# Backward of an adaLN block with a sliding-window decode attention and a gated feed-forward: part of the feed-forward's row sums moved from VectorE to TensorE

## The chip, the cores and the metric

The kernel runs on one core of one Trainium2 chip. The metric is the device time of one execution in microseconds; three executions of the kernel before took 605.77, 607.19 and 608.46 us, so its median is 607.19 us. The engines are named as the profile names them: PE is TensorE (PEld its weight loads), DVE is VectorE, ACT is ScalarE, POOL is GpSimd, SP is SyncE. POOL and SP here mainly issue DMAs.

## The reference, cut to what matters

The forward pass of one token (all tensors bf16, D = 1024, F = 3584, 32 query heads over 4 key/value heads of 128, a cache of 65,536 rows of which only the last W = 4096 are attended to):

```
mod = silu(c) @ w_mod                       -> sa, ca, ga, sb, cb, gb   (1024 each)
h   = layernorm(x) * (1 + ca) + sa
x   = x + ga * (attention(h, last 4096 rows of k, v) @ wo)
h   = layernorm(x) * (1 + cb) + sb
x   = x + gb * ((sigmoid(h @ w_gate) * (h @ w_up)) @ w_down)
```

The kernel must return x and the gradients, for a given grad_out, with respect to x, both caches, wq, wo, w_gate, w_up, w_down, c and w_mod. The gradients of the caches are as large as the caches, 61,440 of 65,536 rows of each head being zero: 120 pieces of about 1 MB of zeros are written, and these are called fills below. The gradients of the weight matrices are outer products of a column and a row, so most of the rest of the output is also plain writing.

In the feed-forward's backward pass the gradient of the hidden input is needed: dh2[j] = sum over f of (w_up[j, f] du[f] + w_gate[j, f] dg[f]), where du and dg are called the dug row. This is the row sum that the change deals with.

## The kernel before, in words

All of the work is written out by hand in one function, in the order in which each engine is to run it; each engine runs its own instructions strictly in that order and waits on semaphores of the others. Nearly all of SBUF is one tile, `arena`, cut by hand with `ar(off, size)`; a piece is used again as soon as its last reader is done, and for a stored piece that is when its DMA has landed.

DMAs leave by two queues: POOL issues most of them (fills, weights, gradients; the queue q0 of the profile), SP a few loads and stores (q1). Both queues run on the same 16 DMA engines. A fill is issued by `zero(n)` at the place where it is called; how many are issued at which place is set by the constants `Z_...` at the head of the file. There are 120 in all, so a fill that one place does not issue is issued at a later one.

The stages in order: modulation and query; scores; sums over the attended rows; the products called b_ps (a stage of 512 large matmuls); the feed-forward; a stage of outer products (`dw_rows`, `dwd`, `dwo`); and the gradients of keys, values, wq and w_mod.

The feed-forward (lines 1009 to 1152) goes over F in NB = 7 blocks q of 512. For each block, w_up and w_gate (2 MB, `load_ug`, two buffers, POOL queue) and w_down (1 MB, `load_wd`, one buffer, SP queue) are loaded. The work of a block is:

- `front(q)`, PE: 32 matmuls multiply the block's weights with the column h2_bf; the sums lie in a PSUM bank `fg` (`gu_ps` in its first half, the feed-forward's output `ffn_ps` in its second).
- `turn(q)`: `gates` (DVE masks and sums the PSUM rows into a column, clears `gu_ps` by a memset, ACT computes two sigmoids); `wd_ttr`: four DVE multiply-and-sum instructions over w_down (line 251); `hh_ops`: three small DVE products; `ffn_mm`, PE: 16 matmuls of w_down; then `load_wd(q + 1)`. `dug_part` ends it: two small DVE products make the dug column, PE spreads it into a row in PSUM (8 transposes, line 1059), and ACT copies that row to SBUF (`dug_b`, line 1060). DVE cannot go on before that copy has ended.
- the loop over j, DVE: eight multiply-and-sum instructions `ttr` of 128x1024 (line 251, out arena), one for each of the eight weight tiles of the block, each multiplied in place with `dug_b`. After the fourth, the first half of block q + 2 is loaded over the tiles that are done; after the eighth, the second half. Fills are issued beside both.

Beside this run 46 side jobs (`tr_unit`, line 910 and 911): eight PE transposes into a PSUM tile and an ACT copy back, for later stages. They are taken from a list by `side()`, one for each j. PE's PSUM tiles for the jobs and for the dug row are two, in turn.

In the last two blocks the gradient of w_down of earlier blocks is made too: `dwd(q, off, outer)` multiplies four rows of 128x1024 with columns, on ACT (`outer_act`) or on DVE (`outer_dve`), and stores 1 MB.

After the last block, in the order of the lines 1146 to 1170: `dwd(4)`, `dw_rows(0, 0)` (a 128x3584 product, stored as 0.9 MB), the column of the feed-forward's output from `ffn_ps`, dh2, `op_ps` (32 small matmuls in the same PSUM bank as `fg`), `dwd(5)`, the layer norm's backward (`layernorm_bwd_col`, with a PE sum over partitions between two DVE steps), `dattn_bf`, its broadcast (`bcast`), and then 64 matmuls with wo (line 1263) that give do. Only when do_bf is there do the eight `dwo` follow, each of which stores 1 MB; the `dw_rows` stand between them.

Of the kernel before, what the change touches and what calls it, by code (L numbers as in the profile page):

```python
# [10 lines left out]
P = 128  # L11
# [45 lines left out]
Z_FFN = [(1, 3), (1, 3), (2, 3), (1, 3), (1, 3), (2, 2), (0, 0)]  # L57
Z_HAND = (1, 1, 1, 0)
Z_ROWS = (1, 1)
@with_exitstack  # L60
def kernel(
# [44 lines left out]
    def vt(shape, name, dt=FP32):  # L106
        return pool.tile(shape, dt, name=name)
# [118 lines left out]
    def new_acc(name="acc"):  # L226
        return new_bank(name)[:, 0:64]
# [95 lines left out]
    def layernorm_bwd_col(dln, ln, rstd, name):  # L323
# [4 lines left out]
        means = total_bcast(part, 2, name + "_means", -1.0 / D)  # L328
# [119 lines left out]
    def heads(w):  # L448
        return w.rearrange("p (n d) -> p n d", d=P)
# [561 lines left out]
    dh2acc = vt([P, NB * KD], "dh2acc")  # L1011
# [6 lines left out]
    gu_ps, ffn_ps = fg[:, 0:256], fg[:, 256:512]  # L1018
# [13 lines left out]
    def gates():  # L1032
        rows_to_cols(gu_t, gu_ps, 8, gu_ps)
        nc.vector.memset(gu_ps, 0.0)
        nc.scalar.activation(out=small["sg"], in_=gu_t[:, 4:8], func=ACT.Sigmoid)
        nc.scalar.activation(out=small["om"], in_=gu_t[:, 4:8], func=ACT.Sigmoid, scale=-1.0)

# [15 lines left out]
    def dug_part(q):  # L1053
        dug = dug_all[:, 8 * q:8 * q + 8]
        mulv(dug[:, 0:4], small["dhh"], small["sg"])
        mulv(dug[:, 4:8], small["dhh"], small["hom"])
        tp = new_tp("tp_dug")
        for i in range(8):
            nc.tensor.transpose(tp[:, i * P:(i + 1) * P], dug[:, i:i + 1].broadcast_to([P, P]), ident_bf[:, :])  # L1059
        return nc.scalar.copy(out=dug_b.rearrange("p (k f i) -> p k f i", k=2, i=4),  # L1060
                              in_=tp.rearrange("p (k i f) -> p k f i", k=2, i=4))
# [44 lines left out]
    rot[:] = [(psum, "mm"), (prq, "rq")]  # L1106
    side(1)
    front(0)
    for n, ins in zip(Z_FOLD[2:], turn(0)):
        zero(n, ins)  # L1110
    side(2)
    for q in range(NB):
        z = Z_FFN[q]
        for j in range(KD):
            w = ug_v[:, q % 2, j // 4, j % 4, :, :].rearrange("p k f -> p (k f)")
            ttr(w, w, dug_b, dh2acc[:, q * KD + j:q * KD + j + 1])
            if j == 2 and q + 1 < NB:
                front(q + 1)
            if len(jobs) > 0:
                side()  # L1120
# [11 lines left out]
        if q == NB - 2:  # L1132
            store()
        zero(z[1])
        if q + 2 < NB:
            turn(q + 1)
        elif q + 1 < NB:
            stores = []
            turn(q + 1, lambda: stores.append(dwd(1, 40, outer_act)))
            stores[0]()  # L1140
            zero(Z_HAND[0])
            dwd(2, 152, outer_dve)()
            zero(Z_HAND[1])
            dug_rows(0)
    dwd(4, 32, outer_dve)()
    zero(Z_HAND[3])
# [3 lines left out]
    rows_to_cols(ffn, ffn_ps, KD, ffn_ps)  # L1150
    dh2 = vt([P, KD], "dh2")
    nc.vector.reduce_sum(out=dh2, in_=dh2acc.rearrange("p (b j) -> p j b", j=KD), axis=AX.X)
# [9 lines left out]
    dwd(5, 152, outer_dve)()  # L1162
    dx1b, m2 = layernorm_bwd_col(dln2, ln2, rstd2, "ln2b")
# [4 lines left out]
    dattn_b = scr  # L1168
    bcast(dattn_bf, KD, dattn_b, "V")
# [99 lines left out]
    dw_rows(0, 1, 16, outer_dve)  # L1269
# [11 lines left out]
    dw_rows(0, 2, 40, outer_dve)  # L1281
    dq_bf = vt([P, HQ], "dq_bf", BF16)
# [6 lines left out]
    zero(Z_ROWS[0])  # L1289
    dwo(3)  # L1290
    dw_rows(0, 5, 40, outer_dve)
    dw_rows(0, 6, 16, outer_dve)
    dwo(0)
# [12 lines left out]
    zero(Z_ROWS[1])  # L1306
# [10 lines left out]
    dw_rows(1, 2, 32, outer_dve)  # L1317
    dw_rows(1, 3, 40, outer_dve)
# [11 lines left out]
    dw_rows(1, 4, 16, outer_dve)  # L1330
    sec(1)
# [5 lines left out]
    dw_rows(1, 6, 40, outer_dve)  # L1337
    dw_rows(1, 7, 16, outer_dve)
# [114 lines left out]
```

## Time and profile before

| what | value |
|---|---|
| median of three executions | 607.19 us (605.77 to 608.46) |
| the profiled execution, device time | 604.81 us |
| its span, first to last instruction | 603.0 us |
| bytes moved by DMA | 246.49 MB, 409 GB/s over the span |
| busy share of the span, PE / DVE / ACT / POOL | 66% / 62% / 40% / 25% |
| feed-forward, from the first `gates` to the last row sum | 313.50 to 446.03 us |

The span lies inside the device time; 1.81 us of it lie around the span. In the views below, a line of the timeline gives start and length in us, engine, line of the kernel, operation, what it writes and reads, the count, and in brackets how long the engine had been idle before it and what ended that. Lines of line groups give the count, then busy time and mean length, then idle time before them. Lines by windows give the window, its length, and for each engine its busy time with the number of instructions, then TensorE's granted clock, the DMA engines' busy share (it can be above 1, as packets overlap) and the rate in GB/s.

### The profile page before, as it was taken

How to read it: one execution, taken by the hardware profiler on the slowest of the kernel's cores; microseconds unless marked ns; L12 is line 12 of the kernel's file. 1: busy time of each engine (PE TensorE's matmuls, PEld its weight loads, DVE VectorE, ACT ScalarE, POOL GpSimd, SP SyncE). 2: the span in 40 equal slices, each digit the busy share in tenths (PEclk: the TensorE clock that was granted, in tenths of full speed). 3: DMA queues.
4: the chain of work that ended last, by engine and by line, in shares of the span. 5: the costliest groups of instructions: out<-in, count | busy, mean ns of one | idle time of the engine just before them, and what ended most of it. 6: DMA issues, size and time to landing. Idle time of an engine off the chain costs nothing.

```text
span 603.0 us, 8913 instructions
## 1 busy us (share of the span) xinstructions
PE 396.1 (66%) x3556; PEld 224.4 (37%) x3556; DVE 371.4 (62%) x677; ACT 240.2 (40%) x382; POOL 151.6 (25%) x253
## 2 busy tenths in 40 slices
PE   3997789999999999979766544554226104665510
PEld 2784434334345456435434333343114104413100
DVE  3756499999411030293738888988696735696750
ACT  3489515557211034112235444554443223754410
POOL 3113113212222122222212323321211615233100
PEclk9997699999999999989987777786567656755555
DMA  8999999999999999999999999999996899999998
GB/s 349 421 418 422 414 453 413 433 431 431 409 427 403 456 435 393 447 430 421 388 414 390 408 411 414 418 414 417 425 408 258 336 417 410 424 416 417 413 414 334
DMA packets 33881, 246.49 MB, mean 409 GB/s; under 512 B 5697, under 2 KB 5697, under 8 KB 18448
## 3 DMA queue, kind: packets, MB, share of 16 engines
q0 software_dynamic: 29424, 225.99, 93.7%
q1 hardware_dynamic: 4368, 19.93, 9.2%
q8 instruction: 28, 0.46, 0.3%
q14 instruction: 13, 0.11, 0.0%
q10 hardware_dynamic: 48, 0.01, 0.0%
HBM read 78.28 MB, written 185.60 MB: 438 GB/s over the span
## 4 chain that ended last, share of the span: by engine, by line
PE 37%; DVE 25%; DMA 17%; issue 9%; ACT 7%; POOL 2%; ACTq 0%; POOLq 0%; DVEq 0%; SPq 0%
PE b_ps L767 16%; DMA arena<-in_B_w_down_dram 9%; DVE arena L234 6%; PE n_ps L710 6%; DMA out_dram<-arena 5%; DVE scr L251 5%; DVE arena L251 4%; DVE arena L247 4%; ACT arena L521 2%; ACT arena L1241 2%; PE t_ps L668 2%; DMA out_dram<-zeros 1%; PE tp_k L500 1%; PE w_ps L463 1%; PE ok L630 1%
## 5 line engine op out<-in xcount | busy, mean ns | idle before, releaser
L767 PE MATMUL b_ps<-arena 128*128 128x512 bf16 x512 | 118.6, 385 | 1.1 <-ACT arena L911 1.1
L911 ACT COPY arena<-tp_side 128x1024 bf16<-128x1024 bf16 x62 | 59.8, 1028 | 55.0 <-PE tp_side L910 55.0
L234 DVE TENSOR_TENSOR arena<-arena 128x2048 bf16<-128x2048 bf16 x64 | 76.5, 1223 | 2.3 <-PE n_ps L710 0.3
L251 DVE CUSTOM_DVE_ANT_0 arena<-arena,scr 128x1024 bf16<-128x1024 bf16 x56 | 64.7, 1222 | 13.4 <-ACT scr L1060 13.4
L767 PEld LDWEIGHTS <-arena 128*128 128x128 bf16 x512 | 49.3, 99 | 59.0 <-issue 5.9
L710 PE MATMUL n_ps<-arena 128*128 128x512 bf16 x256 | 65.6, 378 | 5.8 <-DVE arena L234 4.2
L201 POOL DMA_DIRECT2D out_dram<-out_dram x68 | 33.6, 495 | 116.5 <-PE n_ps L710 38.4
L910 PE MATMUL tp_side<-ident_bf,arena 128*128 128x128 bf16 x496 | 46.7, 253 | 16.0 <-ACT arena L911 7.9
L910 PEld LDWEIGHTS <-arena 128*128 128x128 bf16 x496 | 38.8, 116 | 25.7 <-issue 17.5
L247 DVE TENSOR_SCALAR arena<-arena,h 128x3584 bf16<-128x3584 bf16 (+1 forms) x24 | 28.8, 1201 | 25.8 <-DMA out_dram<-arena 25.7
L710 PEld LDWEIGHTS <-arena 128*128 128x128 bf16 x256 | 24.6, 97 | 41.2 <-issue 15.8
L1237 PE MATMUL ps_kv<-arena 32*128 32x512 bf16 x64 | 24.4, 588 | 20.5 <-DVE arena L255 11.1
L207 POOL DMA_DIRECT2D out_dram<-zeros x45 | 24.9, 559 | 50.4 <-PE q_ps L437 13.7
L251 DVE CUSTOM_DVE_ANT_0 scr<-arena,b1k 128x1024 bf16<-128x1024 bf16 x28 | 34.2, 1223 | 5.4 <-DMA arena<-in_B_w_down_dram 4.9
L1241 ACT ACTIVATE arena<-ps_kv 128x512 bf16<-128x512 f32 x48 | 25.4, 697 | 29.0 <-PE ps_kv L1237 28.8
L243 DVE CAST arena<-b_ps 128x512 bf16<-128x512 f32 x6 | 4.2, 692 | 50.8 <-PE b_ps L767 50.8
L670 ACT CAST arena<-t_ps 128x512 bf16<-128x512 f32 x56 | 30.1, 589 | 12.1 <-PE t_ps L668 12.1
L936 POOL DMA_DIRECT2D arena<-in_B_w_up_dram x14 | 10.8, 774 | 65.7 <-DVE dh2acc L251 38.3
L1060 ACT COPY scr<-tp_dug 128x1024 bf16<-128x1024 bf16 x7 | 7.1, 1012 | 46.0 <-PE tp_dug L1059 46.0
L1024 PE MATMUL fg<-arena,hh_bf 128*32 128x256 bf16 x112 | 5.9, 347 | 29.3 <-DVE hh_bf L234 29.3
L521 ACT COPY arena<-tp_wq 128x1024 bf16<-128x1024 bf16 x23 | 21.4, 1071 | 7.3 <-PE tp_wq L519 7.3
L1059 PE MATMUL tp_dug<-ident_bf,rows_all 128*128 128x128 bf16 x56 | 7.2, 311 | 24.0 <-DVE rows_all L234 24.0
(321 smaller groups left out, 639.5 us busy)
## 6 DMA issues: line engine op xcount, KB each, us to landing
out_dram<-zeros POOLq DMA_DIRECT2D x45, 1024.0 KB, 13.1
out_dram<-arena POOLq DMA_DIRECT2D x35, 1024.0 KB, 10.1
out_dram<-arena POOLq DMA_DIRECT2D x16, 896.0 KB, 9.8
arena<-in_A_wq_dram POOLq DMA_DIRECT2D x8, 1024.0 KB, 21.1
arena<-in_A_wo_dram POOLq DMA_DIRECT2D x8, 1024.0 KB, 12.3
arena<-in_w_mod_dram POOLq DMA_DIRECT2D x7, 1024.0 KB, 18.6
arena<-in_B_w_up_dram POOLq DMA_DIRECT2D x14, 512.0 KB, 9.1
arena<-in_B_w_gate_dram POOLq DMA_DIRECT2D x14, 512.0 KB, 9.6
```

What stands on the lines that cost most here:

```text
L201: ins = nc.gpsimd.dma_start(out=as_rows(region, BIGP).bitcast(FP32), in_=zero_src[:, 0:P * ZW // 4].rearrange("i (p x) -> (i p) x", p=BIGP ...
L207: ins = nc.gpsimd.dma_start(out=region.bitcast(FP32), in_=zeros[:, :])
L234: return nc.vector.tensor_tensor(out=out, in0=a, in1=b, op=op)
L247: return nc.vector.tensor_scalar(out=out, in0=a, scalar1=s1, scalar2=None, op0=op0)
L251: return nc.vector.tensor_tensor_reduce(out=out, in0=w, in1=b, scale=1.0, scalar=0.0, op0=ALU.mult, op1=ALU.add, accum_out=acc)
L521: nc.scalar.copy(out=blk, in_=tp[:, :])
L670: nc.scalar.copy(out=o, in_=ps)
L710: mm = nc.tensor.matmul(nbank[k][:, :], lhsT=k_nat[:, g, t_ * DH:(t_ + 1) * DH], rhs=vp[:, t_ % 2, 4 * k:4 * k + 4, :].rearrange("p h d -> ...
L767: mm = nc.tensor.matmul(bbank[p][k][:, :], lhsT=a4[:, p, h, :], rhs=wo_t[u][:, a, k * 512:(k + 1) * 512], start=(i == 0 and a == 0), stop= ...
L910: nc.tensor.transpose(tp[:, i * P:(i + 1) * P], blk[:, i * P:(i + 1) * P], ident_bf[:, :])
L911: nc.scalar.copy(out=blk if dst is None else dst, in_=tp[:, :])
L1241: nc.scalar.activation(out=o, in_=v, func=ACT.Copy, scale=float(scale))
```

## The change

Of each block's eight row sums, five (`JV = 5`) stay on DVE. For the other three, `turned(q)` transposes each weight tile on PE (24 transposes of 128x128), and ACT copies the result back over the tile in place; `turned_mm(q)` then multiplies the turned tiles with the dug column in 24 matmuls with one output column, which add up in a third part of the bank `fg`. The feed-forward's output is also taken with one-column matmuls (32 for each block in place of 16 of 256 columns), so that it needs no masking at the end. The dug row's copy is shared by ACT and DVE. ACT clears `gu_ps` in place of a DVE memset. `load_wd` goes in two halves of 512 KB, each issued when the half's rows have been used. The side jobs are taken two before `front`, three after it and one in `turn`. The three `dwd` that ACT computed go to DVE. In the part after the loop, `dwd(5)` moves into the layer norm's PE sum, and `dw_rows(0, 1)` ahead of the broadcast. Of the fills, the loop issues 17 and no longer 25, the `dwd` stores have one each (5 in place of 3), and the `dw_rows` eight in place of two.

```diff
-Z_FFN = [(1, 3), (1, 3), (2, 3), (1, 3), (1, 3), (2, 2), (0, 0)]
-Z_HAND = (1, 1, 1, 0)
-Z_ROWS = (1, 1)
+Z_FFN = [(0, 3)] * 5 + [(0, 2)]
+Z_HAND = (1, 1, 1, 1, 1)
+Z_ROWS = (1, 1, 1, 1, 1, 1, 1, 1)
+JV = 5
...
     def gates():
         rows_to_cols(gu_t, gu_ps, 8, gu_ps)
-        nc.vector.memset(gu_ps, 0.0)
         nc.scalar.activation(out=small["sg"], in_=gu_t[:, 4:8], func=ACT.Sigmoid)
         nc.scalar.activation(out=small["om"], in_=gu_t[:, 4:8], func=ACT.Sigmoid, scale=-1.0)
+        nc.scalar.activation(out=gu_ps.rearrange("p (n d) -> p n d", n=2), func=ACT.Copy, scale=0.0,
+                             in_=ident_f.rearrange("p (n d) -> p n d", n=1).broadcast_to([P, 2, P]))
+
+    def turned(q):
+        for j in range(JV, KD):
+            w, tp = ug_flat(q, j), new_tp("tp_ug")
+            for b in range(8):
+                k, i = divmod(b, 4)
+                nc.tensor.transpose(tp[:, b * P:(b + 1) * P], w[:, k * FB + i:k * FB + i + FB - 3:4], ident_bf[:, :])
+            nc.scalar.copy(out=w, in_=tp[:, :])
+
+    def turned_mm(q):
+        for j in range(JV, KD):
+            w = ug_flat(q, j)
+            for b in range(8):
+                nc.tensor.matmul(dh2_ps[:, j - JV:j - JV + 1], lhsT=w[:, b * P:(b + 1) * P],
+                                 rhs=dug_all[:, 8 * q + b:8 * q + b + 1], start=False,
...
-    def ffn_mm(q):
-        for i in range(4):
-            ffn_rows(ffn_ps, small["hh_bf"][:, i:i + 1], heads(wd_v[:, i, :]), q == NB - 1 and i == 3)
+    def ffn_mm(q, i0):
+        for i in (i0, i0 + 1):
+            for k in range(KD):
+                nc.tensor.matmul(ffn_ps[:, k:k + 1], lhsT=wd_v[:, i, k * P:(k + 1) * P],
+                                 rhs=small["hh_bf"][:, i:i + 1], start=False,
...
-        return nc.scalar.copy(out=dug_b.rearrange("p (k f i) -> p k f i", k=2, i=4),
-                              in_=tp.rearrange("p (k i f) -> p k f i", k=2, i=4))
+        nc.scalar.copy(out=o[:, 0, :, :], in_=v[:, 0, :, :])
+        return cp(o[:, 1, :, :], v[:, 1, :, :])
...
-    def turn(q, between=lambda: None):
+    def turn(q):
         gates()
+        turned(q)
+        side()
         wd_ttr(0)
         hh_ops(q)
-        between()
-        first = wd_ttr(1, 2, 3)
-        ffn_mm(q)
+        first = wd_ttr(1)
+        ffn_mm(q, 0)
+        if q + 1 < NB:
+            load_wd(q + 1, 0, 2)
+        wd_ttr(2, 3)
+        ffn_mm(q, 2)
+        if q + 1 < NB:
+            load_wd(q + 1, 2, 2)
         last = dug_part(q)
-        if q + 1 < NB:
-            load_wd(q + 1)
+        turned_mm(q)
         return first, last
...
+        if more:
+            side(2)
+            front(q + 1)
+        side(3 if more else len(jobs))
+        for j in range(JV):
+            w = ug_flat(q, j)
+            ttr(w, w, dug_b, dh2acc[:, q * JV + j:q * JV + j + 1])
             if j == 3:
                 if q + 2 < NB:
                     load_ug(q + 2, 0, 4)
-                zero(z[0])
-                if q == NB - 2:
-                    store = dwd(0, 24, outer_act)
-                if q == NB - 1:
-                    dwd(3, 16, outer_act)()
-                    zero(Z_HAND[2])
+                elif more:
+                    zero(Z_FFN[q][1])
+                    dwd(0, 24, outer_dve)()
+                    zero(Z_HAND[0])
+                else:
+                    dwd(3, 16, outer_dve)()
+                    zero(Z_HAND[3])
         if q + 2 < NB:
             load_ug(q + 2, 4, 4)
+            zero(Z_FFN[q][1])
             turn(q + 1)
-            turn(q + 1, lambda: stores.append(dwd(1, 40, outer_act)))
+        elif more:
+            dwd(1, 40, outer_dve)()
+            zero(Z_HAND[1])
+            turn(q + 1)
             dwd(2, 152, outer_dve)()
...
-    rows_to_cols(ffn, ffn_ps, KD, ffn_ps)
+    cp(ffn, ffn_ps)
...
-    dwd(5, 152, outer_dve)()
-    dx1b, m2 = layernorm_bwd_col(dln2, ln2, rstd2, "ln2b")
+    dx1b, m2 = layernorm_bwd_col(dln2, ln2, rstd2, "ln2b", lambda: dwd(5, 152, outer_dve)())
...
     dattn_b = scr
+    dw_rows(0, 1, 16, outer_dve)
+    zero(Z_ROWS[0])
     bcast(dattn_bf, KD, dattn_b, "V")
```

More of the change, by code (lines that the diff above doesn't have):

```diff
@@ L327, in layernorm_bwd_col @@
         ttr(tmp, dln, ln, part[:, 1:2])
-        means = total_bcast(part, 2, name + "_means", -1.0 / D)
+        ps = new_acc("tot_" + name)
+        nc.tensor.matmul(ps[:, 0:2], lhsT=ones_f[:, :], rhs=part[:, 0:2], start=True, stop=True)
+        gap()
+        means = vt([P, 2], name + "_means")
+        ts(means, ps[:, 0:2], -1.0 / D, ALU.mult)
         dx = vt([P, KD], name + "_dx")
@@ L1092 @@
     B_home = [ar(o, 2) for o in (24, 26, 28, 30)] + [b1k, B_t[5], ar(60, 2), B_t[7]]
-    def turn(q, between=lambda: None):
+    def turn(q):
         gates()
+        turned(q)
+        side()
         wd_ttr(0)
         hh_ops(q)
-        between()
-        first = wd_ttr(1, 2, 3)
-        ffn_mm(q)
+        first = wd_ttr(1)
[6 more added lines that the diff above has]
+            load_wd(q + 1, 2, 2)
         last = dug_part(q)
-        if q + 1 < NB:
-            load_wd(q + 1)
+        turned_mm(q)
         return first, last
     rot[:] = [(psum, "mm"), (prq, "rq")]
-    side(1)
+    side(2)
     front(0)
-    for n, ins in zip(Z_FOLD[2:], turn(0)):
-        zero(n, ins)
-    side(2)
+    zero(Z_FOLD[2])
+    zero(Z_FOLD[3], turn(0)[0])
     for q in range(NB):
[L1113 to L1120, printed above, removed]
+        more = q + 1 < NB
+        if more:
+            side(2)
+            front(q + 1)
[3 more added lines that the diff above has]
+            ttr(w, w, dug_b, dh2acc[:, q * JV + j:q * JV + j + 1])
             if j == 3:
```

36 lines of the change are left out of this document (19 added, 17 removed).

## The prediction

> **What bounds the kernel now.** I read the page first: span, share of the DMA engines, rate by slice; then windows cut at the turns of the feed-forward; then the timeline of one turn and of the stretch behind the loop.
>
> ```profile
> span 603.0 us, 8913 instructions
> ...
> DMA  8999999999999999999999999999996899999998
> GB/s 349 421 418 422 414 453 413 433 431 431 409 427 403 456 435 393 447 430 421 388 414 390 408 411 414 418 414 417 425 408 258 336 417 410 424 416 417 413 414 334
> ```
> ```profile
> core 0: us, PE busy (x) PEld busy (x) DVE busy (x) ACT busy (x) POOL busy (x), PEclk, DMA share, GB/s
> 320.20:338.20 18.00, 10.82 (x136) 8.29 (x136) 15.48 (x33) 10.64 (x13) 7.59 (x12) 0.78 1.13 395
> 374.90:393.30 18.40, 9.87 (x120) 7.24 (x120) 15.66 (x33) 8.71 (x11) 6.00 (x9) 0.69 1.16 415
> 412.00:434.60 22.60, 6.64 (x80) 4.56 (x80) 15.75 (x34) 12.56 (x14) 3.42 (x6) 0.58 1.13 423
> 455.00:475.00 20.00, 11.42 (x172) 7.47 (x172) 15.11 (x41) 8.26 (x10) 8.61 (x8) 0.84 0.60 242
> ...
> 540.00:560.00 20.00, 12.85 (x107) 6.30 (x106) 14.39 (x37) 11.30 (x24) 6.75 (x10) 0.50 1.01 419
> ```
>
> The DMA engines are full nearly throughout, in the feed-forward and behind it too, at about 416 GB/s. The bytes don't change, so what can be gained is time in which they are not full. There is one hole: 455 to 475 us at 242 GB/s, (1 - 242/416) x 20 = 8.4 us idle. DVE is busy for 15.7 of 18.4 us in a turn, so the feed-forward's length is set by a chain through DVE, and its fills are as many as keep the DMA engines full meanwhile.
>
> The hole:
>
> ```profile
> 453.26 0.53 POOL L1085 DMA_DIRECT2D out_dram<-arena  x1 [3.67 <-DVE ln2b_parts L251]
> 459.47 0.53 POOL L1077 DMA_DIRECT2D out_dram<-arena  x1 [5.68 <-DVE arena L247]
> 463.27 0.19 DVE L243 CAST do_bf<-do_ps 128x32 bf16<-128x32 f32 x1 [4.09 <-PE do_ps L1267]
> 465.34 0.61 POOL L1207 DMA_DIRECT2D out_dram<-arena  x1 [5.33 <-DVE arena L247]
> 466.92 4.05 POOL L1207 DMA_DIRECT2D out_dram<-arena  x1 [0.97 <-DVE arena L247]
> ```
>
> The chain from the last row sum through the layer norm to do_bf lets POOL issue one store each at 453.26, 459.47 and 465.34; nothing else is queued.
>
> **The change part by part.** A fill is 1.049 MB, 2.5 us at 416 GB/s. Ahead of the hole's end stand 8 fills fewer in the loop, 2 more beside the `dwd` and 1 more behind `dw_rows(0, 1)`: 5 fewer, 12.6 us of DMA work. The other five move behind the hole, where the engines are full, and cost there what they saved. If the chain up to the hole's end gets S us shorter, the hole becomes 8.4 + 12.6 - S = 21.0 - S, and not less than nothing. No change in time is S = 12.6. So S must be added up.
>
> One turn before, from the dug column to the next:
>
> ```profile
> 375.06 1.04 PE L1059 MATMUL tp_dug<-ident_bf,rows_all 128*128 128x128 bf16 x8 [3.18 <-DVE rows_all L234]
> 377.22 1.23 DVE L251 CUSTOM_DVE_ANT_0 arena<-arena,scr 128x1024 bf16<-128x1024 bf16 x1 [2.15 <-ACT scr L1060]
> 386.39 0.43 DVE L234 TENSOR_TENSOR fg<-fg,rows_all 128x256 f32<-128x256 f32 x1
> 387.41 0.27 DVE L1034 MEMSET fg<- 128x256 f32 x1
> 387.90 1.23 DVE L251 CUSTOM_DVE_ANT_0 scr<-arena,b1k 128x1024 bf16<-128x1024 bf16 x1 [0.22 <-DMA arena<-in_B_w_down_dram]
> 393.35 0.15 DVE L234 TENSOR_TENSOR rows_all<-dhh,hom 128x4 bf16<-128x4 f32 x1
> ```
> ```profile
> L1071 ACT COPY arena<-tp_rows 128x512 bf16<-128x512 bf16 x1 | 0.6, 618 | 0.0
> L243 DVE CAST scr<-bc_ps 128x512 bf16<-128x512 f32 x2 | 1.3, 686 | 0.7 <-PE bc_ps L338 0.7
> ```
> ```profile
> 382.85 5.59 ACT L911 COPY arena<-tp_side 128x1024 bf16<-128x1024 bf16 x6 [3.55 <-PE tp_side L910]
> 385.74 0.61 PE L910 MATMUL tp_side<-ident_bf,arena 128*128 128x128 bf16 x8 [0.31 <-ACT arena L911]
> 396.61 1.08 PE L1024 MATMUL fg<-arena,h_bf 128*32 128x256 bf16 x16
> 494.41 0.38 PE L1300 MATMUL dh_ps<-dattn_bf,arena 128*128 128x1 bf16 x8 [23.64 <-ACT arena L1296]
> ```
>
> DVE's order after the change, counted from the dug column: transposes 1.1, the halves of the copy at 0.62 (ACT) and 0.69 (DVE) side by side, so 1.9 where 2.15 stood; five row sums at a pitch of (386.39 - 377.22)/8 = 1.146 us, 5.7; the gates without the memset, 0.9; from `wd_ttr(0)` to the next dug column 393.50 - 387.90 = 5.6. Sum 14.1; before, the same way, 18.4.
>
> PE and ACT now stand close to it. PE: dug 1.1; 24 one-column matmuls at 0.38/8, slower while the clock is low, to 2.7; two side jobs at about 1.0 to 4.7; `front` 2.0 to 6.7; then three side jobs at ACT's pitch of 5.59/6 = 0.93, copied by 10.2. ACT computes the sigmoids only behind them, at 10.4, while DVE wants them at 9.7: 0.7 us. ACT's clearing of `gu_ps`, which no row shows, lies between the small sigmoids' 0.2 and the half copy's 0.62: 0.4. Then three turned copies and a side job; PE is past that job at 13.8, `ffn_mm(q, 0)` ends at 14.5, the second part at 15.3, and the next dug transposes can start. So 14.8 by DVE, 15.3 by PE. The turning is not free of the path: its cover, DVE's chain, is used up.
>
> The first half of w_down is issued at 14.5 and is needed at 15.3 + 8.5, 9.3 us later; the second at 15.3, needed 11.9 us later.
>
> ```profile
> 374.88 13.00 DMA arena<-in_B_w_down_dram
> ```
> ```profile
> arena<-in_B_w_down_dram SPq DMA_DIRECT2D x1, 512.0 KB, 13.3
> ```
> ```profile
> q1 hardware_dynamic: 23, 0.19, 9.1%
> q1 hardware_dynamic: 121, 0.86, 44.7%
> q1 hardware_dynamic: 139, 0.50, 12.8%
> ```
>
> The first row is a whole load, by the chain of waits; the second is the one half load that the trace prices (issued at 298.15): 13.3 us, no less than the whole. The queue rows are of 374.9 to 380.4, of 380.4 to 388.2 (one whole load: hardly anything for 5.5 us, then the bulk in 7.8) and of 302 to 312 (that half: 139 packets for half the bytes). Bounds: first half 9.4 (5.5 silent and half of 7.8) to 13.3; second half in time to a second whole 13.3 behind the first, 26.6 for the pair. I take 9.4, nearest by bytes, and 13.3 after its own issue, nearest by size. The second is then 1.4 late, and as each late turn also lengthens the next one's window, a turn bears half: 16.0 us. With the first at 13.3, 4 us late, a turn is 17.3; with neither late, 15.3.
>
> By the Trainium skill, "DMA: Bandwidth & Descriptors", section Queues, rings and completion order, a DMA engine takes turns between queues packet by packet, so a half with as many packets as a whole needs as many turns; the 139 packets agree, and by it alone the pair would be nearer 26.6 than 14.
>
> ```profile
> 313.50 0.43 DVE L234 TENSOR_TENSOR fg<-fg,rows_all 128x256 f32<-128x256 f32 x1 [2.09 <-PE fg L1024]
> 446.03 1.67 DVE L247 TENSOR_SCALAR arena<-b1k,hh_all 128x1024 bf16<-128x1024 bf16 x4
> 449.14 0.42 DVE L446 TENSOR_REDUCE ffn<-fg 128x8 f32<-128x256 f32 x1
> 453.86 0.16 DVE L247 TENSOR_SCALAR ln2b_means<-tot_ln2b_means 128x2 f32<-128x2 f32 x1 [0.74 <-PE tot_ln2b_means L296]
> ```
>
> The loop, from the first gates to the end of the last row sum (where the next `dwd` starts), took 446.03 - 313.50 = 132.5 us. After: first turn 6.7 as before (313.50 to 320.2), five at 16.0 = 80.0, the sixth with two `dwd` on DVE 14.1 + 2 x 1.67 = 17.5 (in place of 22.6), and to the last sum 1.9 + 2 x 1.67 + 5.7 = 10.9. Sum 115.1, S = 17.4. Behind the loop: the output's masking (0.43 + 0.42) becomes two small copies, -0.6; `dwd(5)` fills DVE's wait of 0.74, -0.7; `dw_rows(0, 1)` delays the broadcast's copies, whose PSUM tile do waits for, by about 0.5, as most of its length lies beside PE's broadcast. S = 18.2. Both weight loads stand ahead of the turn's three fills, and POOL waits for the last row sum as before (the second half of the weights now for `turned_mm` too, which PE has done at 2.7, ahead of it); SP's queue holds only w_down in the loop, and POOL's three fills and two loads for each 16.0 us: 6.3 MB a turn with w_down, 15.1 us, and the backlog of the three fills issued in the first turn covers the difference.
>
> The hole: 21.0 - 18.2 = 2.8 us in place of 8.4, a gain of 5.6. The profiled execution of before took 604.81 us, 1.81 of them outside its span; it would take 599.2. The median of the runs lies 2.4 above it: 607.19 - 5.6 = 601.6 us.
>
> **The rivals.**
>
> *The halves of w_down set the turn (slower).* The place is DVE's wait at `wd_ttr(2)`. With the pair at 26.6 the second half is 13.9 late, a turn is 15.3 + 7.0 = 22.3 us, the loop about 147, S = -13.8, the hole 34.8: 607.2 + 26.4 = 633.6. It decides from a pair of about 17.5 us on (turn 17.7, +3 us). For it: the 13.3 of the half, its packets. Against: the two halves' packets can follow each other without a second silence of 5.5, and fewer fills compete.
>
> *TensorE sets the turn at its low clock (no change).* A side job took 0.61 at the full clock; at half it is about 1.04, as the dug row's eight. Ten such groups 10.4, `front` 2.2, 56 one-column matmuls 4.3, waits 0.9: 17.6 us, loop 123, S = 10.2, hole 10.8: 609.6.
>
> ```profile
> core 0: us, PE busy (x), PEclk, DMA share, GB/s
> 398.10:405.20 7.10, 4.48 (x64) 1.00 1.25 421
> ```
>
> Against it: here 64 matmuls, 48 of them transposes, held the full clock. By the Trainium skill, "TensorE: Matmul & The Clock Gate", Part 4, transposes don't count as work that opens the clock gate, which would speak for this rival; this row disagrees.
>
> *The hole is filled only in its first half.* POOL's issue of 4.05 us at 466.92 stays, and what the fills cover ends before it. Then about 4 of the 8.4 us stay, a gain of 4.4: 602.8.
>
> **How the numbers follow.** 0.5% is 3 us, about what a measurement can tell from no change. The forecast has 0.52 and the half-filled hole 0.10, both faster; the low clock 0.17, within 0.5%; the halves 0.21, slower. The range: below, neither half late, no hole, and the first turn's 395 GB/s mended (0.9 us): 598. Above, the late first half (loop 121.6, S = 11.7: 608.1) and the low clock: 610. Beyond it lies most of the halves' 0.21. The forecast's own range is 598 to 604.
>
> **What would show it.** In the profile after: turns of 15 to 17 us from dug column to dug column; DVE's wait for w_down below 1.5 us a turn; side jobs at 0.6 us; the rate above 380 GB/s in the 20 us ahead of the first `dwo` stores; no new dip in the feed-forward. Wrong would make it: turns above 17.2 us, or a rate below 400 in the loop, which would be idle time that the fills taken away used to cover.

## The result, and the profile after

The changed kernel takes 599.9 us (median of four executions, 597.81 to 600.98) where the kernel before, run beside it, takes 607.26 us: a ratio of 0.9876, 95% interval 0.9837 to 0.9915. The forecast was 601.6 us, in a range of 598 to 610. The profiled execution took 598.86 us; its forecast was 599.2.

The page of the changed kernel, span and rate by slice:

```profile
span 597.1 us, 9794 instructions
...
DMA  8999999999999999999999999999999999999997
GB/s 348 422 418 420 412 468 393 439 426 427 418 423 409 454 435 394 447 428 428 385 414 415 396 387 398 402 388 424 424 425 373 415 424 424 428 409 426 424 423 306
```

The slices with 258 and 336 GB/s, the 31st and 32nd of before, have become 373 and 415. How many bytes that is, is read from windows that are the same for both kernels (columns as in the prediction's windows: window, length, each engine's busy time, TensorE's granted clock, DMA share, GB/s). First before, then after:

```profile
320.00:440.00 120.00, 59.88 (x732) 43.84 (x732) 99.01 (x205) 62.37 (x76) 35.45 (x56) 0.71 1.13 413
440.00:480.00 40.00, 13.44 (x206) 9.35 (x206) 30.53 (x79) 12.80 (x15) 13.16 (x16) 0.69 0.81 323
480.00:580.00 100.00, 45.97 (x453) 25.43 (x453) 67.06 (x117) 44.35 (x78) 26.34 (x40) 0.55 1.03 416
```
```profile
320.00:440.00 120.00, 79.65 (x1186) 64.06 (x1190) 98.18 (x219) 68.40 (x90) 33.66 (x53) 0.73 1.13 405
440.00:480.00 40.00, 9.92 (x156) 6.59 (x148) 19.78 (x40) 9.89 (x12) 15.14 (x18) 0.63 1.01 401
480.00:580.00 100.00, 45.63 (x445) 25.13 (x445) 62.58 (x110) 42.82 (x77) 26.64 (x39) 0.55 1.04 423
```

The total of bytes is the same, so whoever has moved more by 580 us ends earlier. Against before the change moves 8 x 120 = 0.96 MB less in the first window, 78 x 40 = 3.12 MB more in the second and 7 x 100 = 0.70 MB more in the third: 2.86 MB, or 6.9 us at 416 GB/s. The end gives back about 0.9 us (the last slice has 306 GB/s in place of 334). That leaves 6.0; the spans differ by 5.9. So the whole gain is in the hole, and the feed-forward moves bytes a little more slowly than before.

One turn after the change, by the timeline of DVE, dug column to dug column, and two places of later turns; below it four rows of PE and ACT from the same turn:

```profile
336.99 0.16 DVE L235 TENSOR_TENSOR rows_all<-dhh,hom 128x4 bf16<-128x4 f32 x1
338.86 0.69 DVE L244 COPY scr<-tp_dug 128x512 bf16<-128x512 bf16 x1 [1.72 <-ACT scr L1089]
339.59 1.23 DVE L252 CUSTOM_DVE_ANT_0 arena<-arena,scr 128x1024 bf16<-128x1024 bf16 x1
345.32 0.42 DVE L235 TENSOR_TENSOR fg<-fg,rows_all 128x256 f32<-128x256 f32 x1
346.13 1.21 DVE L252 CUSTOM_DVE_ANT_0 scr<-arena,b1k 128x1024 bf16<-128x1024 bf16 x1
351.56 0.15 DVE L235 TENSOR_TENSOR rows_all<-dhh,hom 128x4 bf16<-128x4 f32 x1
...
377.45 1.23 DVE L252 CUSTOM_DVE_ANT_0 scr<-arena,b1k 128x1024 bf16<-128x1024 bf16 x1 [1.24 <-DMA arena<-in_B_w_down_dram]
380.82 1.23 DVE L252 CUSTOM_DVE_ANT_0 scr<-arena,b1k 128x1024 bf16<-128x1024 bf16 x1 [0.58 <-DMA arena<-in_B_w_down_dram]
383.44 0.16 DVE L235 TENSOR_TENSOR rows_all<-dhh,hom 128x4 bf16<-128x4 f32 x1
```
```profile
337.96 0.82 PE L1059 MATMUL fg<-rows_all,arena 128*128 128x1 bf16 x24
338.64 1.98 PE L915 MATMUL tp_side<-ident_bf,arena 128*128 128x128 bf16 x16
344.26 0.61 PE L915 MATMUL tp_side<-ident_bf,junk 128*128 128x128 bf16 x8 [0.65 <-ACT arena L916]
346.51 0.37 ACT L1041 ACTIVATE fg<-ident_f 128x256 f32<-128x256 f32 x1
```

This turn waits for no load of w_down and takes 14.6 us (336.99 to 351.56). The five turns take 16.9, 14.6, 15.4, 16.5 and 15.8, a mean of 15.8; the waits for w_down make the difference, as in the one that ends at 383.44, with 1.24 and 0.58 us of them.

And the first two `dwo` stores, by the timeline of POOL and of DVE beside it:

```profile
447.54 0.62 POOL L1240 DMA_DIRECT2D out_dram<-arena  x1 [8.55 <-DVE arena L248]
449.12 4.05 POOL L1240 DMA_DIRECT2D out_dram<-arena  x1 [0.97 <-DVE arena L248]
451.91 1.15 DVE L248 TENSOR_SCALAR arena<-arena,h 128x3584 bf16<-128x3584 bf16 x1
452.97 0.19 DVE L244 CAST dq_bf<-dq_ps 128x32 bf16<-128x32 f32 x1
```

POOL's issue of 4.05 us is still there, and what is left of the hole lies beside it: 305 GB/s from 450 to 455 us, (1 - 305/416) x 5 = 1.3 us idle. The issue ends at 453.17, 0.11 us after DVE's last product of an unbroken run and 0.2 us after the start of the first instruction that is no product, the cast of dq_bf. The last experiments follow that up.

### The profile page after: what moved, and what is told of

It reads as the page before. It is cut to its first block, busy times and chain, and to the rows that moved or that the text cites. A ratio compares the mean times of both kernels' runs of the same rounds, so it can differ in the third digit from the quotient of the medians.

```text
span 597.1 us, 9794 instructions
## 1 busy us (share of the span) xinstructions
PE 410.8 (69%) x3979; PEld 243.4 (41%) x4004; DVE 354.1 (59%) x647; ACT 246.7 (41%) x398; POOL 152.7 (26%) x253
## 4 chain that ended last, share of the span: by engine, by line
PE 37%; DVE 24%; DMA 22%; issue 6%; ACT 5%; POOL 1%; ACTq 0%; DVEq 0%; POOLq 0%; SPq 0%
PE b_ps L772 16%; DMA out_dram<-arena 12%; DMA arena<-in_B_w_down_dram 9%; DVE arena L248 6%; DVE arena L235 6%; PE n_ps L715 6%; DVE scr L252 4%; DVE arena L252 3%; ACT arena L526 2%; PE t_ps L673 2%; PE tp_k L505 1%; PE w_ps L468 1%; PE ok L635 1%; PE do L1296 1%; PE tp_side L915 1%
## 5 line engine op out<-in xcount | busy, mean ns | idle before, releaser
L772 PE MATMUL b_ps<-arena 128*128 128x512 bf16 x494 | 116.4, 384 | 2.5 <-ACT arena L916 1.1
L1270 PE MATMUL ps_kv<-arena 32*128 32x512 bf16 x64 | 24.4, 588 | 27.4 <-DVE arena L256 16.1
L715 PEld LDWEIGHTS <-arena 128*128 128x128 bf16 x256 | 24.6, 97 | 41.2 <-issue 15.8
L252 DVE CUSTOM_DVE_ANT_0 arena<-arena,scr 128x1024 bf16<-128x1024 bf16 x35 | 40.8, 1219 | 0.2
L1270 PEld LDWEIGHTS <-arena 32*128 32x128 bf16 x64 | 6.9, 117 | 43.6 <-issue 42.8
L1052 PE MATMUL tp_ug<-ident_bf,arena 128*128 128x128 bf16 x168 | 13.0, 223 | 14.0 <-ACT arena L1053 10.4
L1334 PE MATMUL dh_ps<-dattn_bf,arena 128*128 128x1 bf16 x48 | 2.1, 167 | 28.0 <-ACT arena L1330 28.0
## 6 DMA issues: line engine op xcount, KB each, us to landing
out_dram<-zeros POOLq DMA_DIRECT2D x45, 1024.0 KB, 14.5
arena<-in_A_wo_dram POOLq DMA_DIRECT2D x8, 1024.0 KB, 12.6
```

The source lines that it names most:

```text
L252: return nc.vector.tensor_tensor_reduce(out=out, in0=w, in1=b, scale=1.0, scalar=0.0, op0=ALU.mult, op1=ALU.add, accum_out=acc)
L715: mm = nc.tensor.matmul(nbank[k][:, :], lhsT=k_nat[:, g, t_ * DH:(t_ + 1) * DH], rhs=vp[:, t_ % 2, 4 * k:4 * k + 4, :].rearrange("p h d -> ...
L772: mm = nc.tensor.matmul(bbank[p][k][:, :], lhsT=a4[:, p, h, :], rhs=wo_t[u][:, a, k * 512:(k + 1) * 512], start=(i == 0 and a == 0), stop= ...
L1270: nc.tensor.matmul(ps[:, :], lhsT=rows[r, t8 * P:(t8 + 1) * P], rhs=bd[r, :], start=True, stop=True, tile_position=(32 * tc_, 0))
```

## The experiments

The first four experiments ran on one chip (kernel before: 606.32 us), the next three and the first of the last section on another (606.05), the last four on a third (606.62). Ratios are to the kernel before on the same chip.

### The fills alone

The kernel before, with only the places of its fills changed to those of the new kernel (where a place exists in both):

```diff
-Z_FFN = [(1, 3), (1, 3), (2, 3), (1, 3), (1, 3), (2, 2), (0, 0)]
-Z_HAND = (1, 1, 1, 0)
-Z_ROWS = (1, 1)
+Z_FFN = [(0, 3)] * 5 + [(2, 1), (0, 0)]
+Z_HAND = (1, 1, 1, 1)
+Z_ROWS = (1,) * 8
```

> The kernel before with nothing changed but the places of the fills (17 in the loop, one beside each dwd store, eight beside the dw_rows). Theory (the hole is 8.4 + 2.5 k - S, k fills moved behind it, S what the chain got shorter): k = 5, S = 0, so 21.0 us idle in place of 8.4, and the time is about 619.9 us, 12.6 above the kernel before; the turns stay at 18.4 us and the rate in the loop falls to about 365 GB/s. Rival (it is the fills put beside the dw_rows that close the hole): 5 us or more below the kernel before, without any work on TensorE.

Measured: 614.56 us, ratio 1.0136 (1.0104 to 1.0168), 8.2 us slower. By windows:

```profile
320.00:440.00 120.00, 59.23 (x732) 43.49 (x732) 100.61 (x209) 63.84 (x78) 30.68 (x48) 0.70 1.02 368
440.00:480.00 40.00, 13.61 (x206) 9.38 (x206) 29.25 (x77) 11.36 (x13) 16.37 (x20) 0.68 0.87 342
```

The turns stay at 18.1 us, and the DMA engines now idle in the loop: 45 GB/s less than before over 120 us is 5.4 MB, 13 us. The hole gets only 19 x 40 = 0.76 MB better. Moving the fills by itself loses, 8.2 us where my theory had 12.6; the rival that they alone close the hole falls.

### The shorter turn alone

The changed kernel, with its fills laid out as before:

```diff
-Z_FFN = [(0, 3)] * 5 + [(0, 2)]
-Z_HAND = (1, 1, 1, 1, 1)
-Z_ROWS = (1, 1, 1, 1, 1, 1, 1, 1)
+Z_FFN = [(0, 4), (0, 4), (0, 5), (0, 4), (0, 4), (0, 4)]
+Z_HAND = (0, 1, 1, 1, 0)
+Z_ROWS = (0, 0, 1, 0, 1, 0, 0, 0)
```

> The changed kernel with the fills where the kernel before had them (25 in the loop, three and two). Theory: k = 0 and S of 10 or more leave no hole, since 8.4 - S is below nothing; the loads have more ahead of them in the queues, so turns grow from 15.8 to about 17.5 us, the rate of the loop goes back to about 410 GB/s, and the time is that of the changed kernel, 598 to 601. Rival (the moved fills close the hole): the hole comes back to 5 us or more, about 604 to 606.

Measured: 604.78 us, ratio 0.997 (0.9956 to 0.9983). My theory had the turns (17.5 us in the mean of five) and the loop's rate (407 GB/s) right and the time wrong: the rival's hole is there. Windows of the timeline, then the chain of waits' totals between 312 and 450 us (waiter, what it waited for, us in total, times, longest), then three places of the timeline:

```profile
320.00:440.00 120.00, 69.86 (x1065) 55.86 (x1062) 91.35 (x191) 58.93 (x80) 35.37 (x56) 0.70 1.15 407
440.00:480.00 40.00, 22.17 (x274) 16.53 (x273) 20.90 (x62) 18.39 (x21) 11.66 (x12) 0.67 0.84 334
```
```profile
PE fg L1029 <- DMA arena<-in_B_w_gate_dram: 18.2, 6, 4.9
DVE scr L252 <- DMA arena<-in_B_w_down_dram: 3.1, 3, 1.9
```
```profile
440.67 1.93 ACT L1100 COPY arena<-tp_rows 128x1024 bf16<-128x1024 bf16 x2 [10.93 <-DMA out_dram<-arena]
451.94 0.19 DVE L244 COPY kb_col<-op_ps 128x32 f32<-128x32 f32 x1 [6.21 <-PE op_ps L1189]
464.29 0.19 DVE L244 CAST do_bf<-do_ps 128x32 bf16<-128x32 f32 x1 [5.78 <-PE do_ps L1300]
```

The hole is there again, at 334 GB/s over the window where before had 323, and do_bf comes at 464.29 us, 1.0 us later than before (the loop began 1.9 us later, at 315.42). The turns begin short (16.5, 15.9, 15.5 us) and end long (18.9, 20.6, 18.9): with the longer queue of fills in front of them the weight loads land later (w_gate 13.4 us after its issue, the median from 320 to 440 us, where the changed kernel has 9.1), and PE waits 18.2 us for w_gate (2.1 before, by the same view). The last row sum still ends 6.6 us earlier than before, at 439.39; behind the loop that is lost too, as ACT waits 10.93 us for a store to land whose place it writes over. So the time that DVE saves can't be laid by as a backlog of DMA work ahead of the hole: each fill queued early also makes the loads and stores late on which the chain waits. Without the fills moved, the work taken off DVE is worth 1.5 us in all.

### w_down whole

The changed kernel, with the load of w_down issued in one piece behind the second half's use:

```diff
         ffn_mm(q, 0)
-        if q + 1 < NB:
-            load_wd(q + 1, 0, 2)
...
-            load_wd(q + 1, 2, 2)
+            load_wd(q + 1)
```

> The changed kernel with w_down loaded whole, after the second half of its use, as before. Theory: the issue moves from 14 to 15.3 us after the dug column and the whole lands 13.0 to 13.3 later, so DVE waits at its first row and a turn takes 17.5 us or more; S falls by 8 to 9 and the time rises by 8 to 10 us over the changed kernel, to about 609. Rival (a half takes as long as a whole, so halves gain nothing): turns of 15.8 us and the time of the changed kernel within 2 us.

Measured: 612.24 us, ratio 1.009 (1.0056 to 1.0124), 12 us above the changed kernel. The waits of DVE for w_down:

```profile
DVE scr L252 <- DMA arena<-in_B_w_down_dram: 19.5, 6, 5.6
```

With the halves the same line of the changed kernel reads:

```profile
DVE scr L252 <- DMA arena<-in_B_w_down_dram: 6.5, 8, 2.1
```

13 us of waiting lie in the chain, and nearly all of it reaches the end: the theory's direction, by 12 us where it had 8 to 10, and the rival falls. The halves are needed, though a half lands hardly sooner after its issue than a whole: the listing of DMA issues of the changed kernel (KB each, median us from issue to landing) has

```profile
arena<-in_B_w_down_dram SPq DMA_DIRECT2D x14, 512.0 KB, 11.9
```

That median is of three landings, 8.7 to 12.7 us. By the ends of DVE's waits the six wholes of this run took 9.9 to 18.0 us, four of them 9.9 to 12.7. A half also has as many packets as a whole: from 312 to 430 us the SP queue has 1728 packets for 12 halves in the changed kernel, and 864 for six wholes in the kernel before, 144 for each. So what the halves bring is most likely the earlier issue of the first one; no run has the early issue without the halves.

### All row sums on DVE

The changed kernel, with nothing turned over:

```diff
-JV = 5
+JV = 8
```

> The changed kernel with all eight row sums on DVE and nothing turned (JV = 8); halves, moved fills and the rest stay. Theory: a turn takes 14.1 + 3 x 1.146 = 17.6 us, S is about 3, the hole 18, the time about 617 us. Rival (the halves and the other small parts made the loop shorter, not the turned tiles): turns of 16 us and 600 to 603 us.

Measured: 616.01 us, ratio 1.0163 (1.013 to 1.0197), close to the theory's 617. The dug columns come 18.0 us apart (319.78, 337.78, 355.78, 373.78, 391.79, 409.79), no wait for w_down is left, and the loop starves the DMA engines as with the fills alone:

```profile
320.00:440.00 120.00, 56.61 (x784) 45.05 (x785) 106.39 (x214) 47.98 (x68) 29.01 (x45) 0.66 1.06 366
```

So the three turned row sums are what shortens the turn; the other edits of the loop without them leave it at 18.0.

### Six row sums on DVE

```diff
-JV = 5
+JV = 6
```

> Six row sums on DVE, two turned tiles (JV = 6). Theory (DVE, PE and the w_down loads are about level in a turn): DVE has 1.15 us more, PE and ACT about 1.2 us less ahead of the first w_down issue, so DVE's waits for w_down get shorter and turns stay between 15.5 and 16.5 us; time within 2 us of the changed kernel. Rival A (DVE alone sets the turn): turns of 17 us, 604 to 606. Rival B (TensorE and ScalarE set it): turns of 14.7 us, and no dip is left: 597 to 599.

Measured: 602.04 us, ratio 0.9931 (0.9915 to 0.9948). Five turns take 17.2, 15.7, 15.7, 16.3 and 15.7 us, a mean of 16.1, and the waits for w_down fall to 2.1 us: one DVE sum more (1.15 us a turn) mostly stands where DVE had waited for w_down. The turns are the theory's, the time isn't quite: 2.1 us above the changed kernel, 3.3 by the ratios. do_bf comes 3.2 us later than in the changed kernel: 1.5 us from the five turns, 1.0 from the sixth (18.9 us for 17.9) and 1.0 from behind it, less 0.3 by which the first dug column came earlier.

### Some fills back into the loop

The changed kernel, with 20 and not 17 fills in the loop:

```diff
-Z_FFN = [(0, 3)] * 5 + [(0, 2)]
+Z_FFN = [(0, 4), (0, 4), (0, 4), (0, 3), (0, 3), (0, 2)]
-Z_ROWS = (1, 1, 1, 1, 1, 1, 1, 1)
+Z_ROWS = (1, 1, 1, 1, 1, 0, 0, 0)
```

> The changed kernel with three of the moved fills back in the loop (4, 4, 4, 3, 3, 2), taken from the last three places beside the dw_rows; those ahead of and in the hole stay. Theory (the chain is tied to the DMA queue by the landings it waits for, and only work issued behind the last loads and close to the hole covers it): turns of the first blocks grow to 16.5 to 17.5 us, the hole stays as small as in the changed kernel, and the time is within 1.5 us of it, 598.5 to 601.5. Rival (each fill left in the loop takes its share of the gain away): about half of what putting back eight fills lost, 602 to 603.

Measured: 599.03 us, ratio 0.9879 (0.9862 to 0.9896): the same as the change, though do_bf comes 8.7 us later, at 454.15. Between five and eight fills moved behind the loop the time is flat: as long as enough work is queued at the hole, it doesn't matter when the hole comes. In this trace POOL's second store issue wasn't long:

```profile
457.80 0.61 POOL L1240 DMA_DIRECT2D out_dram<-arena  x1 [0.97 <-DVE arena L248]
```

DVE runs the same products beside it as in the changed kernel, to within 0.02 us. So an issue can be held there, and need not be; why one is and another is not stays open.

### The two moves behind the loop undone

The changed kernel, with `dwd(5)` ahead of the layer norm and `dw_rows(0, 1)` behind do again:

```diff
-    dx1b, m2 = layernorm_bwd_col(dln2, ln2, rstd2, "ln2b", lambda: dwd(5, 152, outer_dve)())
+    dwd(5, 152, outer_dve)()
+    dx1b, m2 = layernorm_bwd_col(dln2, ln2, rstd2, "ln2b")
...
-    dw_rows(0, 1, 16, outer_dve)
-    zero(Z_ROWS[0])
     bcast(dattn_bf, KD, dattn_b, "V")
```

> The changed kernel with dwd(5) ahead of the layer norm's backward and dw_rows(0, 1), with its fill, behind the do matmuls, as before. Theory: dattn_bf comes about 0.7 us later, and 2 MB of DMA work are issued about 4 us later; the DMA engines run dry for 1 to 3 us ahead of it; time 1 to 3 us above the changed kernel. Rival (nothing depends on that order): within 0.5 us.

Measured: 599.78 us, ratio 0.9899 (0.9876 to 0.9923), not to be told from the change (by the ratios 1.4 us above it, with intervals that overlap). do_bf comes at 444.99 us, 0.5 earlier than with the two moves, not later, and the DMA engines don't run dry ahead of it: 430 GB/s from 435 to 440 us. The theory's mechanism falls, and no worth of the two moves is shown.

### What holds POOL's issue

The row sum of the mask (0.17 us of DVE), which DVE otherwise reaches only at 489.49 us (505.00 in the kernel before), moved to behind the first four `dwd` products. The run of products is then broken about 3 us before the cast of dq_bf ends it; that is the 2.9 us of the expectations. First in the changed kernel:

```diff
     dwd(6, 32, outer_dve)()
+    nc.vector.reduce_sum(out=in_group, in_=mask.rearrange("p (g r) -> p g r", g=G), axis=AX.X)
     dq_ps = new_acc("dq_ps")
...
-    nc.vector.reduce_sum(out=in_group, in_=mask.rearrange("p (g r) -> p g r", g=G), axis=AX.X)
```

> The changed kernel with one small sum on DVE (in_group, 128x4 from 128x32, otherwise computed later) moved between the four products of dwd(6) and those of dwo(5). In both kernels POOL's issue of the second dwo store takes 4.05 us, and it ends when DVE's row of products is first broken by another kind of instruction. Theory (POOL is held by DVE's back-to-back products): the issue ends at the break, in 1.5 to 2.2 us, and the remaining dip of the DMA rate (450 to 455 us, 305 GB/s, 1.4 us idle) shrinks; time 0 to 1.4 us below the changed kernel. Rival (the 4 us belong to POOL's own instructions): still 4.05 us, no change.

Measured: 596.37 us, ratio 0.9849 (0.9828 to 0.987). That is 3.5 us below the changed kernel's 599.9, but the two were not run side by side. And in its trace the issue takes 0.62 us and is over at 449.51, ahead of the row sum at 450.09: it was not held at all. So four kernels went to one chip: the changed kernel again,

> The changed kernel as it is, on one chip with the three below, so that all stand against the same runs of the kernel before. Theory of the hold: GpSimd's second issue of a dwo store, at about 449 us, lasts 4.05 us in this kernel because VectorE then runs scalar products one behind the other, and it ends 0.2 us after the first instruction of another kind (the cast of dq_bf) begins. So the 4.05 us issue is there again, ends 0.2 us behind the start of that cast, and the rate of 450 to 455 us is again about 300 GB/s: 598 to 601 us, ratio 0.985 to 0.992. Rival (the 4.05 us was an accident of one execution): no issue over 1.5 us between 440 and 460 us.

the same with the row sum moved,

> The changed kernel with the mask's row sum (0.17 us of VectorE) moved to right behind the first four dwd products, 2.9 us earlier in VectorE's order. Theory of the hold: no issue of GpSimd there lasts over 1.5 us, since VectorE now comes to another kind of instruction 1.4 us behind the start of the second store's issue; 1 to 4 us less than the changed kernel on the same chip, 596 to 598.5 us. Rival (the earlier difference came from the chip or from chance): within 1 us of the changed kernel.

the kernel before with the row sum moved and nothing else,

> The kernel before with that one row sum moved to the same place, nothing else. Theory of the hold: GpSimd's 4.05 us issue at 466.9 us falls to at most 1.5 us, and up to 2.6 us of the 8.4 us hole goes: 603 to 605.5 us (1 to 3 us less than before). Rival A (the hole of before is a want of work in the queue, and the late start of the first stores sets it; the hold costs nothing beside it): within 0.7 us of the kernel before. Rival B (the hold is the hole's cause, all of it): 5 us or more less than before.

and the moved row sum together with 20 fills in the loop (the two diffs above in one):

> The row sum moved as above and, beside it, the fills of the changed kernel laid out so that 20 and not 17 lie in the feed-forward loop and 5 and not 8 behind it. Theory (what closes the hole is work queued behind it, and with 17 fills and no hold it is closed already; three fills more in the loop make its turns longer and take nothing from the hole): the same as the version with the row sum alone or up to 2 us slower, 596.5 to 599 us. Rival (the loop at 397 GB/s still lacks work, so three more fills there pay): 1 us or more faster than with the row sum alone, 594 to 595.5 us.

| kernel | median, us | lowest to highest | ratio, 95% |
|---|---|---|---|
| before | 606.62 | 603.85 to 608.27 | |
| before, row sum moved | 603.88 | 603.03 to 606.25 | 0.9969 (0.9951 to 0.9987) |
| changed | 598.55 | 597.41 to 599.42 | 0.987 (0.9844 to 0.9897) |
| changed, row sum moved | 596.94 | 595.95 to 597.44 | 0.9843 (0.982 to 0.9867) |
| changed, row sum moved, 20 fills in the loop | 596.01 | 595.49 to 597.66 | 0.9833 (0.9809 to 0.9858) |

The timelines, POOL beside DVE: the changed kernel; the same with the row sum moved; the kernel before with it moved; the last of the table.

```profile
448.82 4.05 POOL L1240 DMA_DIRECT2D out_dram<-arena  x1 [0.97 <-DVE arena L248]
452.67 0.18 DVE L244 CAST dq_bf<-dq_ps 128x32 bf16<-128x32 f32 x1
```
```profile
448.28 0.61 POOL L1240 DMA_DIRECT2D out_dram<-arena  x1 [0.97 <-DVE arena L248]
449.48 0.17 DVE L1309 TENSOR_REDUCE in_group<-rows_all 128x4 f32<-128x32 f32 x1
```
```profile
468.26 1.67 DVE L247 TENSOR_SCALAR arena<-b1k,hh_all 128x1024 bf16<-128x1024 bf16 x4
468.63 1.41 POOL L1207 DMA_DIRECT2D out_dram<-arena  x1 [0.97 <-DVE arena L247]
469.84 0.18 DVE L1277 TENSOR_REDUCE in_group<-rows_all 128x4 f32<-128x32 f32 x1
```
```profile
456.26 1.41 POOL L1240 DMA_DIRECT2D out_dram<-arena  x1 [0.97 <-DVE arena L248]
457.46 0.18 DVE L1309 TENSOR_REDUCE in_group<-rows_all 128x4 f32<-128x32 f32 x1
460.58 4.15 POOL L1106 DMA_DIRECT2D out_dram<-arena  x1 [0.17 <-DVE dq_bf L244]
462.94 1.67 DVE L248 TENSOR_SCALAR arena<-scr,kb_col 128x1024 bf16<-128x1024 bf16 x4
```

In the kernel before with the row sum moved, the issue is held for 1.41 us and no longer 4.05: it ends at 470.04, 0.2 us after the row sum begins, 0.11 after the last product of the run ends (468.26 + 1.67 = 469.93). In the last kernel it is the same (457.67), and the next run of products holds another issue, 4.15 us, which ends at 464.73, again 0.12 after the run's end (464.61). In all nine traces in which the 4.05 us issue occurs it ends 0.19 to 0.21 us after the cast of dq_bf begins. That settles when it ends: POOL's issue, once held, comes through only when DVE's run of products stops.

What begins a hold isn't shown. In the changed kernel with the row sum moved the issue is over at 448.89 us, ahead of the row sum at 449.48: the expectation (no issue over 1.5 us) came true, but not because the row sum ended a hold. And the changed kernel has its 4.05 us issue again, as expected, but 382 GB/s and not about 300 from 450 to 455 us, 0.4 us of idle time in place of 1.3.

What it costs: in the kernel before 2.7 us by the medians and 1.9 by the ratio (0.8 to 3.0 by its interval), and in the changed one, held against not held, 1.6 us on the same chip (two ranges that meet only at 597.4). In the kernel before the hole goes from 323 to 331 GB/s over its 40 us, 0.8 us of work, and is still a hole: the rival that the hold is all of it falls, and so does the one that it costs nothing. In the changed kernel with the row sum moved nothing of the hole is left. First the changed kernel on that chip, then with the row sum moved; the 15 GB/s over 40 us are 1.4 of the 1.6 us:

```profile
440.00:480.00 40.00, 9.12 (x160) 6.21 (x152) 19.78 (x40) 10.11 (x13) 15.14 (x18) 0.67 1.03 410
```
```profile
320.00:440.00 120.00, 80.76 (x1190) 65.72 (x1194) 98.49 (x221) 68.72 (x90) 33.66 (x53) 0.74 1.14 402
440.00:480.00 40.00, 8.94 (x165) 6.24 (x157) 19.78 (x41) 11.16 (x14) 12.48 (x18) 0.67 1.05 425
```

By the Trainium skill, "SBUF — State Buffer", section SBUF: two separate sides, GpSimd writes the descriptors of its DMAs through a port pair that VectorE takes for itself during some of its operations, and GpSimd is then locked out of it. The hold and its end agree with that; that it is a port that is held, no run here shows. The figure of the section A bandwidth-pool intuition that's wrong, a block until about 0.115 us after VectorE's end, agrees with the 0.11 and 0.12 here. The page has the lock end with the instruction; here it lasted through a run of nine products of about 0.4 to 1.1 us each, and the issue came through in none of the seams between them.

The row sum moved with 20 fills in the loop is the fastest kernel, by 2.5 us against the change. Against the row sum alone it is 0.9 us faster, by ranges that overlap: neither my theory (0 to 2 us slower) nor its rival (1 us or more faster) is shown. Its loop moves 408 GB/s where the one with 17 fills moves 402, which may be work that was lacking there; without the row sum moved, 17 and 20 fills have 405 both. Its window from 440 to 480 us has 421 GB/s in spite of the 4.15 us hold, so there a hold cost little.

## Why the prediction was right, by its own steps

- **The bound, and the hole.** Right. The gain is the hole: 3.12 MB more there, 0.96 less in the loop and 0.70 more behind, 2.86 in all. The prediction left the hole at 2.8 us; 1.3 us stayed.
- **The formula, hole = 21.0 - S.** Right as an account, but S is not free of the fills. S, counted from the first gates to do_bf, was 18.1 where I had 18.2: 17.7 in the loop (313.84 to 428.6 us, 114.8 long, for 115.1), and 0.4 behind it. With each run's own S the formula gives -5.5 us for the change (measured -7.4), +10.7 for the fills alone (S = 1.9; measured +8.2), -0.9 for the shorter turn alone (0.9; -1.5), +7.5 for w_down whole (5.1; +5.9) and +11.6 for all sums on DVE (1.0; +9.7). It is too high each time, by 0.6 to 2.5 us; in four of the five the rate from 480 to 580 us is 421 to 424 GB/s and not 416, which is worth 1.2 to 1.9 us of that. What I had wrong is that the shorter turn alone should have closed the hole. It did not: with the fills as before S was 0.9 and not 18, because the chain then waits for landings. The parts alone are worth -1.5 and +8.2 us, together -7.4. Moving the fills is not the price of the change but the half of it that turns a shorter chain into time.
- **The turn, 16.0 us.** Right in the sum (15.8), by errors that cancel, so in part by luck. DVE's own chain took 14.6, for 14.1: the halves of the dug row's copy hardly lie side by side, as DVE starts its own only behind ACT's (the row with 1.72 <-ACT), 2.0 to 2.4 us to the first sum in place of 1.9. The five sums (5.73, for 5.7), the gates (0.81, for 0.9) and the w_down part (5.6, for 5.6) came as worked out. TensorE's 15.3 was too much: the 24 one-column matmuls took 0.82 us, where I had allowed 1.6.
- **The halves of w_down.** Mis-sized. Priced at 9.4 us for the first and 13.3 for the second; the firsts took 11.5 to 13.1 us (the last of them 8.7), the seconds 12.7 to 14.2. The first was issued 12.7 to 14.3 us into the turn, earlier than the 14.5 that I had, and still it was the late one: DVE waits 0.9 to 2.1 us for it in four of five turns, and 0.2 to 0.6 more for the second, where I had only the second late, by 1.4. The load of half the bytes takes nearly as long as a whole, and the two overlap. By the Trainium skill, "DMA: Bandwidth & Descriptors", section Queues, rings and completion order, the turns that a queue gets go by packets. That bears on the 11.9 of a half beside the 13.0 of a whole, with 144 packets in each; but the pair didn't take the 26.6 us that the prediction drew from that rule alone, and the rival built on it, 633.6 us, did not come.
- **TensorE at its low clock.** Did not come as the limit of a turn, though the low clock did: in the turn shown the two side jobs behind the dug row take 0.99 us each (1.98 for both) and those from 344.26 us on 0.61, so the sign that I had named, side jobs at 0.6 us, came in part. The slow ones lie beside DVE's row sums, and the granted clock is 0.73 over 320 to 440 us. With nothing but transposes the clock did come up: in the run of the shorter turn alone TensorE ran nothing else from 441.7 to 450.4 us, and its granted clock was 0.50 up to 446 us and 1.00 from 448 on. The terms of this rival add up to 17.8 us and not 17.6, which makes its time 610.6.
- **The hole filled only in its first half.** Its mechanism did come, 4.05 us at 449.12, and the kernel in which that issue wasn't held prices it at 1.6 us; the rival had 1.2 (602.8 less 601.6).
- **Behind the loop, -0.8.** 0.4 us came, and not by the moves: undoing both made do_bf 0.5 us earlier.
- **The loop's rate.** The prediction took the loop's 15.1 us of DMA work in a turn of 16.0 to be covered by the backlog of the first turn. 405 GB/s in place of 413 over 120 us, 2.3 us, is the term that is missing from the sum; the better rate behind the hole, 423 for 416, 1.7 us, nearly pays for it, and was not foreseen either. The whole loop has 404 GB/s, but 320 to 400 us has 397, under the 400 that I had named as a sign of being wrong. That the time came out within 2 us is luck as far as these two cancel.

## What to carry to other kernels

Where the DMA engines bound a kernel, a shorter chain is worth only what it takes out of their idle time: find the hole, and move independent transfers behind the loop so that they are queued when the hole comes. Here one half alone lost 8.2 us and the other gained 1.5, and together they gained 7.4, so try such a pair together, and read both from windows that are the same in both kernels. Look for long DMA issues on GpSimd beside an unbroken run of VectorE products: in two kernels here an instruction of another kind, put between them from elsewhere in the order, let a held issue through.

## What the runs showed that I had not expected

- A GpSimd DMA issue, mostly 0.5 to 0.9 us, can last 4.05 us, and its end is set by VectorE: 0.11 us after a run of products ends. One small instruction put into the run cut it to 1.41 us in the kernel before, which then took 1.9 us less of 606.6 by the ratio (0.8 to 3.0).
- The same issue beside the same products passed in 0.61 us in three traces (20 fills in the loop; twice with the row sum moved, before DVE came to it) and took 4.05 in nine; what decides it is not shown.
- A queue kept full by early fills delays the loads that share it: 18.2 us of waiting for w_gate with eight fills more in the loop, and a store that ACT waited 10.93 us for.
